# Attention with packed tokens: scores, packed values and projection in eight array tiles of 64 rows by 32 columns

## The chip, the cores and the metric

The program runs on one core of a Trainium2 chip. The metric is device time in microseconds of one execution; less is better. TensorE (PE) does matmuls from a stationary operand (loaded by LDWEIGHTS, shown as PEld) and a moving one; VectorE (DVE), ScalarE (ACT) and GpSimd (POOL) do the rest; SyncE (SP) issues the DMAs.

## The reference

Three layers follow one another, all in f32. B = 8 batches, 8 heads, S = 576 tokens, head size d = 64, 32 packed queries per head.

```
# 1 attention through 32 packed tokens per head
pp  = softmax(p k^T / 8) v            # 32 x 64 per head
x   = softmax(q pp^T / 8) pp          # 576 x 64 per head; heads side by side: 576 x 512
# 2 mixture of 4 causal attention experts (size 64), the best 2 of 4 by x w_gate
out = sum_e gate_e * (causal_softmax((x wq_e)(x wk_e)^T / 8) (x wv_e)) wo_e
# 3 token-shifted feed-forward, y = out, y' = out one token earlier
xk  = mu_k y + (1 - mu_k) y';  xr = mu_r y + (1 - mu_r) y'
res = sigmoid(xr w_r) * (relu(xk w_k)^2 w_v)
```

The kernel never forms x. As x = a2 pp with a2 = softmax(q pp^T / 8), it multiplies the packed values by the weights of layer 2 first (pp w_in, with w_in = all wq, wk, wv and w_gate side by side, 772 columns) and applies a2 to that.

## The kernel before

Heads are worked on in two groups of four (g = 0, 1) per batch; four heads times 32 packed tokens fill 128 partitions. `front(b, g)` is one such group, 16 in all, as a generator of nine steps:

- loads of p, k, v, q on the SP queue (`load`, L231-248);
- scores s1 of the packed queries with the keys (`scores_pair`, the matmul of L224), their maximum (L265) and exp (L270);
- five PE transposes of the result (L277);
- packed values: for each of 5 chunks of 128 keys, 2 matmuls (L286), each for a pair of heads (64 stationary columns, 128 moving ones);
- multiplication by 1/sum and by `bmask` (L293), which zeroes what belongs to the other head of the pair; a PE transpose (L299) gives ppT;
- scores s2 of q with the packed values (`scores_pair` again), a DVE transpose (L306), maximum, subtraction, exp;
- projection: ppT times the weights `wa`, in two column ranges of 512 and 260, 2 matmuls each (L319); ACT writes the rounded result PWh (L325), DVE the rest PWl (L326);
- sums, division and a transpose of a2.

A matmul of the pair form has 128 contracted rows and 64 stationary columns: two heads' 64 features stand on the two halves of the partitions. For s1, p is stored apart, with zeros where the other head's features are; for the packed values the cross products are computed and `bmask` drops them. The two pairs (jj = 0, 1) write PSUM partitions 0-63 and 64-127, so they are two column tiles of the array. `big()` gives a PSUM tile of 2 banks (2 of these), `one()` one of 1 bank (4 of these).

Behind `front` come `values` (L363) and `project` (L418), which apply a2, and per expert `soft` (L477: causal scores, DVE L489, ACT L493), `turn` (PE transposes L516, L523, copied by L211/L213), `pair_out` (L559, L569). `fold` (L706) prepares products of wo with w_k and w_r meanwhile: the weights come in 64-bit form and DVE, ACT and POOL decode them (L622 to L657). Layer 3 follows: `rstage` (L865), `kstage` (L885), `vunit` (L926).

Order: every step of every generator has a due time (constants such as FRONT_T, G1_T, SOFT_T; a batch is 20 units). The steps are called in the order of their due times; some have a priority; then a planner with a model of the instructions' lengths fixes the order on each engine. Each engine runs its list in order.

Of the kernel before, what the change touches and what calls it, by code (L numbers as in the profile page):

```python
# [9 lines left out]
F32 = mybir.dt.float32  # L10
# [4 lines left out]
ALU = mybir.AluOpType  # L15
# [36 lines left out]
def f32(ap):  # L52
    return ap.bitcast(F32)
# [3 lines left out]
def kernel(  # L57
# [3 lines left out]
):  # L61
    nc = tc.nc
    P = 128
    B, NG, _, _, S = q.shape
    D, NPK = p.shape[3], p.shape[6]
    DM, DFF = w_k.shape
    NE, HD = 4, wo.shape[1] // 4
    SH = S // 2
    NT = (S + P - 1) // P
    TAIL = S - (NT - 1) * P  # L70
    QB = 256
# [1 line left out]
    NDT = DM // P  # L73
    QK = 2 * HD * NE
    NCB = S // NPK
    VG = HD * NE + NE
    NQK = QK + VG
    assert w_in.shape == (DM, NQK) and out.shape[2] == DM == NG * 4 * D
    assert (P, S, D, NPK, HD, NE, NT, TAIL) == (128, 576, 64, 32, 64, 4, 5, 64)
    SC = 1.0 / math.sqrt(D)  # L80

# [4 lines left out]
    const = ctx.enter_context(tc.tile_pool(name="const", bufs=1))  # L86
# [7 lines left out]
    def nm(s):  # L94
        uid[0] += 1
        return f"{s}_{uid[0]}"

    def big():
        return psb.tile([P, 1024], F32, tag="big", name=nm("big"))

    def one():
        return pso.tile([P, 512], F32, tag="one", name=nm("one"))

    ident = const.tile([P, P], F32, name="ident")
# [7 lines left out]
    bmask = const.tile([P, 2, D], F32, name="bmask")  # L112
    nc.vector.memset(bmask, 0.0)
    for h in range(4):
        nc.vector.memset(bmask[32 * h : 32 * h + 32, h % 2, :], 1.0)
    lower = const.tile([P, NE, NE], F32, name="lower")
    nc.vector.memset(lower, 0.0)
    for e in range(1, NE):
# [25 lines left out]
    if True:  # L144
# [6 lines left out]
        ex_cm, ex = pool("ex", 2, "left")  # L151
        bt_cm, bt = pool("bt", 1, "left")

        wa = wa_pool.tile([P, NDT, NQK], F32, name="wa")

# [39 lines left out]
                yield  # L195

        def load_wa():
            for c in range(0, NDT, 2):
                nc.sync.dma_start(
                    wa[:, c : c + 2, :], w_in[P * c : P * c + 2 * P].rearrange("(c p) n -> p c n", p=P)  # L200
                )

        def halves(ap):
            return ap.rearrange("p (h n) -> p h n", h=2)
# [12 lines left out]
        def pool_tt(o, x, y, op):  # L217
            nc.gpsimd.tensor_tensor(o, x, y, op=op)  # L218

        def scores_pair(lhs, rhs):  # L220
            ps = big()
            for hf in range(2):
                for jj in range(2):
                    nc.tensor.matmul(  # L224
                        ps[64 * jj : 64 * jj + 64, 512 * hf : 512 * hf + SH],
                        lhs[:, 64 * jj : 64 * jj + 64],
                        rhs[:, jj, SH * hf : SH * hf + SH],
                        start=True, stop=True,
                    )
            return halves(ps)[:, :, :SH]  # L230

        def load(b, gs):

            for g in gs:
                pT = pTs[(b * NG + g) % 2]
                nc.sync.dma_start(pT, p[b, g].rearrange("h d j i n -> (h d) (j i n)"))
                kT = ld.tile([P, 2, S], F32, tag="kT", name=nm("kT"))
                nc.sync.dma_start(kT, k[b, g])
                loaded[b, g] = [pT, kT]
            for g in gs:  # L240
                vn = vns[(b * NG + g) % 2]
                nc.sync.dma_start(
                    vn[:, : NT - 1, :], v[b, g, : (NT - 1) * P].rearrange("(c p) x -> p c x", p=P)
                )
                nc.sync.dma_start(vn[TAIL:, NT - 1, :], v[b, g, (NT - 1) * P :])
                qT = ld.tile([P, 2, S], F32, tag="qT", name=nm("qT"))
                nc.sync.dma_start(qT, q[b, g])
                loaded[b, g] += [vn, qT]

        def front(b, g):  # L250
# [9 lines left out]
                load(b, (g,) if b else range(NG))  # L260
            pT, kT, vn, qT = loaded.pop((b, g))
            yield
            s1 = scores_pair(pT, kT)
            mx = sm.tile([P, 1], F32, tag="mx1", name=nm("mx1"))
            nc.vector.tensor_reduce(mx, s1, op=ALU.max, axis=AX.XY)  # L265
            nb = sm.tile([P, 1], F32, tag="nb1", name=nm("nb1"))
# [30 lines left out]
            yield  # L297
            ps = one()
            nc.tensor.transpose(ps[:, :P], pp, ident)  # L299
# [13 lines left out]
            )  # L313
            nc.scalar.activation(st, st, AF.Exp, scale=SC)
            yield
            ps = big()
            for lo, hi in ((0, QK), (QK, NQK)):
                for jj in range(2):
                    nc.tensor.matmul(  # L319
                        ps[64 * jj : 64 * jj + 64, lo:hi],  # L320
                        ppT[:, 64 * jj : 64 * jj + 64],
                        wa[:, 2 * g + jj, lo:hi],
                        start=True, stop=True,
                    )
# [728 lines left out]
def layout(q, k, v, p, moe_w_gate, moe_wq, moe_wk, moe_wv, moe_wo,  # L1053
           moe2_mu_k, moe2_mu_r, moe2_w_k, moe2_w_v, moe2_w_r):

    import numpy as np

    b, h, _, d = q.shape  # L1060
    ne, dm, hd = moe_wq.shape

    def features(a):
        return a.reshape(b, h // 4, 2, 2, -1, d).transpose(0, 1, 3, 5, 2, 4)

    cols = []
    for e in range(0, ne, 2):
        cols += [moe_wq[e], moe_wq[e + 1], moe_wk[e], moe_wk[e + 1]]
    apart = np.zeros((b, h // 4, 2, d, 2, 2, p.shape[2]), p.dtype)
    for x in range(2):  # L1070
        apart[:, :, x, :, :, x] = features(p)[:, :, x]
    arrays = {
        "q": features(q).reshape(b, h // 4, 2 * d, 2, -1),
        "k": features(k).reshape(b, h // 4, 2 * d, 2, -1),
        "v": v.reshape(b, h // 4, 4, -1, d).transpose(0, 1, 3, 2, 4).reshape(b, h // 4, -1, 4 * d),
        "p": apart,
        "w_in": np.concatenate(cols + list(moe_wv) + [moe_w_gate], axis=1),
        "wo": moe_wo.reshape(ne * hd, dm).T,
        "mu": np.stack([moe2_mu_k, moe2_mu_r]).reshape(2, -1, 128).transpose(2, 0, 1), "w_k": moe2_w_k, "w_v": moe2_w_v, "w_r": moe2_w_r,
    }  # L1080
    arrays = {n: np.ascontiguousarray(a) for n, a in arrays.items()}
    return {n: a.view(np.int64) if a.dtype == np.float64 else a for n, a in arrays.items()}
# [19 lines left out]
```

## Time and profile before

| | |
|---|---|
| median of 3 runs | 822.84 us (822.81 to 822.85) |
| profiled execution | 823.26 us |
| its span | 821.5 us |
| PE busy | 791.0 us, 96% |
| DVE, ACT, POOL busy | 483.9, 480.2, 381.4 us |
| DMA moved | 147.72 MB |

The span goes from the first instruction to the last. Busy time counts an engine's instructions, overlaps once. A chain of waits follows the work that ended last back to its start, at each step to what released it or to the instruction before it on its engine. A matmul's duration runs until its results are written, so matmuls overlap: the pace is read from a run of many. An f32 matmul leaves two records (each LDWEIGHTS and MATMUL), an f32 PE transpose one. `128*64` is rows times columns of the array used. A few matmul records are missing from the trace.

### The profile page before, as it was taken

The numbers are of one execution on the slowest core, as the hardware profiler recorded it, in microseconds if no ns is written. First come the engines' busy times: TensorE is split into PE (matmuls) and PEld (weight loads), VectorE is DVE, ScalarE is ACT, GpSimd is POOL, SyncE is SP. The second block draws the span as 40 slices with busy tenths as digits, with TensorE's granted clock in tenths as the row PEclk, the third lists the DMA queues.
The fourth block names the chain that finished last, engine by engine and source line by source line (L and its number), as shares of the span: only waits on it lengthen the run. The fifth ranks groups of instructions, "written<-read, shape, count | busy, mean of one in ns | idle before, by whom it ended". The sixth has DMA issues, their size and how long they took to land.

```text
span 821.5 us, 13912 instructions
## 1 busy us (share of the span) xinstructions
PE 791.0 (96%) x4800; PEld 639.8 (78%) x4800; DVE 483.9 (59%) x1177; ACT 480.2 (58%) x1093; POOL 381.4 (46%) x490
## 2 busy tenths in 40 slices
PE   7698999999999999999899999999999999999998
PEld 5385968869687796868678888888888888888886
DVE  3989785886868757556856778787584111111111
ACT  2367777687676877778844624232678765556400
POOL 4567666394764735225700407171166443433610
PEclk9899999999999999999999999999999999999999
DMA  9865464634636254112834967785979655555511
GB/s 318 264 158 172 136 199 125 189 125 136 212 106 185 88 138 154 49 50 60 242 106 170 361 243 246 221 264 182 340 260 311 210 198 171 184 162 188 153 66 51
DMA packets 90085, 147.72 MB, mean 180 GB/s; under 512 B 6816, under 2 KB 61600, under 8 KB 87712
## 3 DMA queue, kind: packets, MB, share of 16 engines
q1 hardware_dynamic: 89872, 146.84, 56.2%
q8 instruction: 38, 0.62, 0.3%
q14 instruction: 31, 0.25, 0.1%
q10 hardware_dynamic: 144, 0.00, 0.0%
HBM read 87.04 MB, written 50.33 MB: 167 GB/s over the span
## 4 chain that ended last, share of the span: by engine, by line
PE 76%; DVE 11%; ACT 5%; DMA 4%; issue 2%; POOL 1%; SPq 0%; DVEq 0%; ACTq 0%; POOLq 0%
PE one L926 24%; PE big L885 8%; PE one L885 8%; PE one L559 5%; PE big L418 4%; PE big L865 4%; PE one L865 4%; PE one L706 3%; PE one L363 3%; PE one L477 3%; PE one L516 3%; PE big L224 2%; ACT ms L493 2%; DVE ms L489 2%; DMA raw<-in_w_k_dram 2%
## 5 line engine op out<-in xcount | busy, mean ns | idle before, releaser
L931 DVE TENSOR_TENSOR ring<-one,ring 128x512 f32<-128x512 f32 x36 | 24.9, 691 | 167.1 <-PE one L926 162.4
L926 PE MATMUL one<-wvh,yh 128*128 128x512 f32 x288 | 112.0, 389 | 0.0
L926 PE MATMUL one<-wvl,yh 128*128 128x512 f32 x288 | 112.0, 389 | 0.0
L926 PE MATMUL one<-wvh,yl 128*128 128x512 f32 x288 | 112.0, 389 | 0.0
L493 ACT ACTIVATE ms<-ms,nb 64x64 f32<-64x64 f32 (+4 forms) x160 | 89.5, 560 | 29.2 <-DVE nb L489 26.9
L211 ACT COPY tb<-one 64x128 f32<-64x128 f32 (+5 forms) x208 | 64.6, 356 | 30.3 <-PE one L523 28.0
L218 POOL TENSOR_TENSOR yl<-yvh,yh 128x1024 fp32r<-128x1024 f32 (+1 forms) x24 | 49.4, 2073 | 45.6 <-ACT yh L911 27.7
L637 POOL TENSOR_TENSOR dcx<-dcx,dcu 128x256 f32<-128x256 f32 x40 | 30.6, 764 | 78.2 <-DVE dcu L631 76.8
L559 PE MATMUL one<-tb,vg 128*64 128x320 f32 (+4 forms) x448 | 62.6, 367 | 4.3 <-ACT tb L211 3.4
L926 PEld LDWEIGHTS one<-wvh,yh 128*128 128x128 f32 x288 | 54.1, 188 | 11.3
L926 PEld LDWEIGHTS one<-wvh,yl 128*128 128x128 f32 x288 | 54.1, 188 | 11.3
L926 PEld LDWEIGHTS one<-wvl,yh 128*128 128x128 f32 x288 | 54.1, 188 | 11.0
L489 DVE CUSTOM_DVE_ANT_0 ms<-one,mstrip 64x64 f32<-64x64 f32 (+3 forms) x128 | 51.6, 421 | 15.8 <-PE one L477 13.5
L516 PE MATMUL one<-ident,ms 128*128 128x128 f32 x320 | 55.0, 280 | 2.7 <-ACT ms L493 1.1
L559 PEld LDWEIGHTS one<-tb,vg 128*64 128x64 f32 x448 | 36.9, 138 | 26.5 <-ACT tb L211 6.0
L218 POOL TENSOR_TENSOR yl<-yvl,yh 128x1024 fp32r<-128x1024 f32 x16 | 38.3, 2402 | 37.1 <-issue 19.3
L516 PEld LDWEIGHTS one<-ident,ms 128*128 128x128 f32 x320 | 37.8, 141 | 17.0 <-issue 6.8
L218 POOL TENSOR_TENSOR dt<-cb 128x192 f32<-128x192 f32 (+1 forms) x48 | 29.4, 640 | 35.3 <-ACT p L871 15.5
L477 PE MATMUL one<-ks,qs 128*128 128x64 f32 (+3 forms) x128 | 40.9, 346 | 1.5 <-DMA ks<-ks 1.3
L477 PE MATMUL one<-kl,qs 128*128 128x64 f32 (+3 forms) x128 | 39.2, 306 | 0.0
L1048 ACT ACTIVATE ring<-ring 128x1024 f32<-128x1024 f32 x18 | 19.1, 1060 | 33.7 <-DMA ring<-rscr 33.7
L657 POOL TENSOR_TENSOR wl<-wc,wh 128x256 fp32r<-128x256 f32 x48 | 35.4, 753 | 0.5
(208 smaller groups left out, 2106.4 us busy)
## 6 DMA issues: line engine op xcount, KB each, us to landing
yscr<-y SPq DMA_DIRECT2D x48, 384.0 KB, 3.6
dl<-dscr SPq DMA_DIRECT2D x40, 256.0 KB, 6.1
yvh<-yscr SPq DMA_DIRECT2D x10, 1024.0 KB, 5.5
kT<-in_k_dram SPq DMA_DIRECT2D x16, 576.0 KB, 4.2
qT<-in_q_dram SPq DMA_DIRECT2D x16, 576.0 KB, 5.4
rscr<-rr SPq DMA_DIRECT2D x12, 768.0 KB, 4.8
ring<-rscr SPq DMA_DIRECT2D x36, 256.0 KB, 2.9
out_dram<-ring SPq DMA_DIRECT2D x36, 256.0 KB, 3.2
```

Source lines behind the costliest of these rows:

```text
L211: nc.scalar.copy(o, x)
L218: nc.gpsimd.tensor_tensor(o, x, y, op=op)
L418: nc.tensor.matmul(ps[:, 512 * hf : 512 * hf + SH], ww[:, g, :], xx[:, g, :], start=i == 0, stop=i == 3 * NG - 1,)
L477: nc.tensor.matmul(ps[:, po : po + kn], qs[:, i * P : i * P + P], keys[:, ko : ko + kn], start=x == 0, stop=x == 1,)
L489: nc.vector.tensor_tensor_reduce(halves(mv) if last else mv, sv, halves(mk) if last else mk, op0=ALU.add, op1=ALU.min, scale=-SC, scalar=3 ...
L493: nc.scalar.activation(mv, mv, AF.Exp, bias=nb[p0:], scale=-1.0, accum_out=bat["sums"][p0:, i, e : e + 1],)
L516: nc.tensor.transpose(ps[:, at + j * P : at + (j + 1) * P], ms[:, j * P : (j + 1) * P], ident)
L559: nc.tensor.matmul(av[64 * ee : 64 * ee + 64, qo - lo : hi - lo], vg[:, j, HD * (2 * ep + ee) : HD * (2 * ep + ee + 1)], tslice(tabs[ee], ...
L657: nc.gpsimd.tensor_sub(l, x, f32(h))
L865: nc.tensor.matmul(po, dx[:, NS * t + s, t0 : t0 + P], wpart("r", s, wx, t), start=n == 0, stop=n == 3 * KT - 1,)
L885: nc.tensor.matmul(po.rearrange("p (b n) -> p b n", b=2), wpart("k0" if f < 4 else "k1", s, wx, t)[:, f % 4 * P : f % 4 * P + P], dx[:, :, ...
L926: nc.tensor.matmul(ps, a[:, f, P * t : P * t + P], wres["v"][b][:, f, :], start=n == 0, stop=n == 3 * NFT - 1,)
```

## The change

A helper `eight(lhs, rhs, n)` takes the place of `scores_pair` and of the projection's loop. It issues eight matmuls with 64 contracted rows and 32 stationary columns: for each of the 4 heads j and each half hf of the partitions, one that writes PSUM partitions 32j to 32j + 31, in the bank of that half. The two halves of the partitions hold the two halves of the moving columns (tokens, or columns of the weights: 772 = 2 x 386), and the same 64 features of the head. So p is laid out twice, one copy per half, without zeros; q and k are laid out with tokens 0-287 on the lower and 288-575 on the upper partitions; `w_in` likewise. The packed values are computed per head in four column tiles (128 rows x 32 columns, 64 moving columns), 20 matmuls instead of 10, and nothing has to be masked: `bmask` goes, and the multiplication by 1/sum writes the 64 values twice, so that the transpose gives ppT with both copies. Due times and priorities are as before.

```diff
+        def eight(lhs, rhs, n):
             ps = big()
-            for hf in range(2):
-                for jj in range(2):
+            for j in range(NH):
+                for hf in range(2):
+                    r = slice(64 * hf, 64 * hf + 64)
                     nc.tensor.matmul(
-                        ps[64 * jj : 64 * jj + 64, 512 * hf : 512 * hf + SH],
-                        lhs[:, 64 * jj : 64 * jj + 64],
-                        rhs[:, jj, SH * hf : SH * hf + SH],
+                        ps[NPK * j : NPK * j + NPK, 512 * hf : 512 * hf + n],
+                        lhs[r, NPK * j : NPK * j + NPK],
+                        rhs[r, j, :],
                         start=True, stop=True,
                     )
-            return halves(ps)[:, :, :SH]
+            return halves(ps)[:, :, :n]
...
-            s1 = scores_pair(pT, kT)
+            s1 = eight(pT, kT, SH)
...
             for c in range(NT):
-                for jj in range(2):
+                for j in range(NH):
                     nc.tensor.matmul(
-                        ps[64 * jj : 64 * jj + 64, :P],
-                        aT[:, c, 64 * jj : 64 * jj + 64],
-                        vn[:, c, P * jj : P * jj + P],
+                        ps[NPK * j : NPK * j + NPK, :D],
+                        aT[:, c, NPK * j : NPK * j + NPK],
+                        vn[:, c, D * j : D * j + D],
                         start=c == 0, stop=c == NT - 1,
                     )
-            pp = fr.tile([P, P], F32, tag="pp", name=nm("pp"))
-            nc.vector.scalar_tensor_tensor(
-                pp, ps[:, :P], ri, bmask.rearrange("p a d -> p (a d)"),
-                op0=ALU.mult, op1=ALU.mult,
+            pp = fr.tile([P, 2, D], F32, tag="pp", name=nm("pp"))
+            nc.vector.tensor_scalar(
+                pp, ps[:, :D].unsqueeze(1).to_broadcast([P, 2, D]), ri, None, op0=ALU.mult
             )
...
-            s2 = scores_pair(ppT, qT)
+            s2 = eight(ppT, qT, SH)
...
-            for lo, hi in ((0, QK), (QK, NQK)):
-                for jj in range(2):
-                    nc.tensor.matmul(
-                        ps[64 * jj : 64 * jj + 64, lo:hi],
-                        ppT[:, 64 * jj : 64 * jj + 64],
-                        wa[:, 2 * g + jj, lo:hi],
-                        start=True, stop=True,
-                    )
-            nc.scalar.copy(bat["PWh"][:, g, :], ps[:, :NQK])
-            nc.vector.tensor_sub(bat["PWl"][:, g, :], ps[:, :NQK], f32(bat["PWh"][:, g, :]))
+            ps = eight(ppT, wa[:, NH * g : NH * g + NH, :], NW)
+            nc.scalar.copy(halves(bat["PWh"][:, g, :]), ps)
+            nc.vector.tensor_sub(halves(bat["PWl"][:, g, :]), ps, halves(f32(bat["PWh"][:, g, :])))
```

The tiles that are loaded change shape, not size: pT 128 x 128, kT and qT 128 x 4 x 288 instead of 128 x 2 x 576, wa 128 x 8 x 386 instead of 128 x 4 x 772. `bmask` and its five memsets are removed.

## Rows read from the trace of the kernel before

**Rows 1.** Busy time, share of the span and instructions of each engine (page, part 1).
```profile
PE 791.0 (96%) x4800; PEld 639.8 (78%) x4800; DVE 483.9 (59%) x1177; ACT 480.2 (58%) x1093; POOL 381.4 (46%) x490
```

**Rows 2.** Busy us by stage: length, PE, PEld, DVE, ACT, POOL, clock, DMA share, GB/s.
```profile
20.00:61.00 41.00, 32.62 (x240) 25.50 (x236) 36.83 (x92) 20.65 (x50) 24.96 (x41) 0.92 0.71 213
61.00:103.00 42.00, 39.16 (x303) 31.02 (x302) 34.79 (x105) 30.15 (x88) 28.58 (x43) 1.00 0.51 153
103.00:145.00 42.00, 41.80 (x324) 32.71 (x321) 31.12 (x95) 30.39 (x89) 29.04 (x49) 1.00 0.54 159
145.00:187.00 42.00, 41.52 (x323) 31.34 (x323) 34.22 (x108) 30.53 (x91) 26.67 (x42) 1.00 0.52 155
187.00:229.00 42.00, 41.65 (x336) 33.36 (x335) 33.93 (x108) 31.42 (x91) 25.23 (x45) 1.00 0.60 173
229.00:271.00 42.00, 42.00 (x343) 35.55 (x339) 30.90 (x97) 29.21 (x85) 25.70 (x44) 1.00 0.51 151
271.00:313.00 42.00, 40.68 (x334) 33.81 (x334) 25.16 (x79) 29.68 (x88) 19.95 (x34) 1.00 0.47 134
313.00:355.00 42.00, 40.07 (x313) 31.69 (x313) 28.04 (x90) 33.72 (x99) 15.10 (x25) 1.00 0.26 72
...
430.00:822.00 392.00, 386.95 (x1726) 319.79 (x1726) 171.67 (x248) 187.14 (x253) 146.22 (x96) 1.00 0.63 210
```

**Rows 3.** Chain of waits by line, of 0-21, 103-313, 145-187, 187-229, 313-375 us.
```profile
by line: DMA raw<-in_w_k_dram 51.4%; DMA vn<-in_v_dram 35.5%; SPq L238 4.0%; SPq L236 3.9%; SPq L671 1.8%; issue 1.5%
...
by line: PE one L559 12.5%; PE big L418 10.6%; PE one L706 10.1%; PE one L477 7.6%; PE one L363 7.1%; PE big L224 6.8%; PE one L516 6.7%; PE one L286 4.1%; DVE ms L489 3.4%; ACT ms L493 3.2%; PE big L319 2.8%; DMA raw<-in_w_r_dram 2.7%; PE 
...
by line: DMA raw<-in_w_r_dram 13.3%; PE one L559 9.0%; PE one L477 8.3%; PE big L224 5.3%; PE one L516 4.6%; DVE ms L489 4.0%; issue 3.8%; PE one L363 3.7%; PE big L319 3.4%; DVE kl L437 3.4%; PE one L706 3.4%; PE one L286 3.0%; ACT ms L493
...
by line: PE one L559 15.2%; PE big L418 15.1%; PE one L706 10.6%; PE big L224 8.0%; PE one L477 7.8%; PE one L516 7.7%; PE one L363 7.2%; PE one L286 5.9%; DVE ms L489 5.6%; PE big L477 3.8%; PE big L319 3.4%; PE one L523 2.1%; PE big L569 
...
by line: PE one L559 12.9%; PE big L418 10.3%; PE one L477 7.6%; DVE ms L489 7.2%; ACT ms L493 6.9%; PE one L363 6.1%; PE one L516 6.1%; PE big L224 5.4%; ACT tb L211 5.1%; DMA ks<-ks 3.7%; DVE PWl L326 2.8%; ACT PWh L325 2.4%; PE big L569 
```

**Rows 4.** Pieces of that chain, 187-229 and 313-375 us: start us, us, what.
```profile
194.59 0.55 PE big L277 x5
...
202.79 1.24 PE one L286 x20
...
211.21 1.12 PE big L224 x8
...
216.69 1.45 PE big L319 x8
...
316.56 1.45 PE big L319 x8
...
351.54 1.24 PE one L286 x20
```

**Rows 5.** TensorE in order of time, 75.4-77 us: start us, us, what, count.
```profile
75.22 0.39 PE L559 MATMUL one<-tb,vg 128*64 128x128 f32 x4
75.90 1.19 PE L224 MATMUL big<-kT,pT 128*64 128x288 f32 x8 [0.29 <-DVE nb L489]
```

**Rows 6.** VectorE groups by shape: busy us, mean ns, idle before.
```profile
L326 DVE TENSOR_TENSOR PWl<-big,PWh 128x772 fp32r<-128x772 f32 x16 | 15.2, 949 | 0.1
...
L431 DVE TENSOR_TENSOR l<-big,qs 128x576 fp32r<-128x576 f32 x16 | 12.1, 756 | 9.7 <-ACT qs L430 9.4
...
L293 DVE SCALAR_TENSOR_TENSOR pp<-one,ri,bmask 128x128 f32<-128x128 f32 x16 | 5.5, 344 | 1.2 <-PE one L286 0.9
```

**Rows 7.** DMA issues (page, part 6): count, KB each, us to landing.
```profile
kT<-in_k_dram SPq DMA_DIRECT2D x16, 576.0 KB, 4.2
```

**Rows 8.** 103-430 us, lines L224, L286, L319 alone: us, PE (count), PEld (count).
```profile
103.00:430.00 327.00, 26.48 (x176) 11.68 (x176) 0.99 0.46 135
...
103.00:430.00 327.00, 13.83 (x214) 11.18 (x210) 0.99 0.46 135
...
103.00:430.00 327.00, 18.21 (x96) 5.82 (x96) 0.99 0.46 135
```

More of the change, by code (lines that the diff above doesn't have):

```diff
@@ L63 @@
     P = 128
-    B, NG, _, _, S = q.shape
-    D, NPK = p.shape[3], p.shape[6]
+    B, NG, _, NH, SH = q.shape
+    D, NPK = p.shape[2] // 2, p.shape[4]
+    S = 2 * SH
     DM, DFF = w_k.shape
     NE, HD = 4, wo.shape[1] // 4
-    SH = S // 2
     NT = (S + P - 1) // P
@@ L77 @@
     NQK = QK + VG
-    assert w_in.shape == (DM, NQK) and out.shape[2] == DM == NG * 4 * D
+    NW = NQK // 2
+    assert w_in.shape == (P, NG * NH, NW) and out.shape[2] == DM == NG * NH * D
     assert (P, S, D, NPK, HD, NE, NT, TAIL) == (128, 576, 64, 32, 64, 4, 5, 64)
@@ L111 @@
     )
[L112 to L115, printed above, removed]
     lower = const.tile([P, NE, NE], F32, name="lower")
@@ L152 @@
         bt_cm, bt = pool("bt", 1, "left")
-        wa = wa_pool.tile([P, NDT, NQK], F32, name="wa")
+        wa = wa_pool.tile([P, NG * NH, NW], F32, name="wa")
         qss = [ex.tile([P, TAIL + 2 * S], F32R, name=f"qs{x}", bufs=1) for x in range(2)]
@@ L197, in load_wa @@
         def load_wa():
-            for c in range(0, NDT, 2):
-                nc.sync.dma_start(
-                    wa[:, c : c + 2, :], w_in[P * c : P * c + 2 * P].rearrange("(c p) n -> p c n", p=P)
-                )
+            for c in range(0, NG * NH, NH):
+                nc.sync.dma_start(wa[:, c : c + NH, :], w_in[:, c : c + NH, :])
         def halves(ap):
@@ L235, in load @@
                 pT = pTs[(b * NG + g) % 2]
-                nc.sync.dma_start(pT, p[b, g].rearrange("h d j i n -> (h d) (j i n)"))
-                kT = ld.tile([P, 2, S], F32, tag="kT", name=nm("kT"))
+                nc.sync.dma_start(pT, p[b, g].rearrange("d j n -> d (j n)"))
+                kT = ld.tile([P, NH, SH], F32, tag="kT", name=nm("kT"))
                 nc.sync.dma_start(kT, k[b, g])
@@ L245, in load @@
                 nc.sync.dma_start(vn[TAIL:, NT - 1, :], v[b, g, (NT - 1) * P :])
-                qT = ld.tile([P, 2, S], F32, tag="qT", name=nm("qT"))
+                qT = ld.tile([P, NH, SH], F32, tag="qT", name=nm("qT"))
                 nc.sync.dma_start(qT, q[b, g])
@@ L298, in front @@
             ps = one()
-            nc.tensor.transpose(ps[:, :P], pp, ident)
+            nc.tensor.transpose(ps[:, :P], pp.rearrange("p x d -> p (x d)"), ident)
             ppT = fr.tile([P, P], F32, tag="ppT", name=nm("ppT"))
@@ L315, in front @@
             yield
-            ps = big()
-            for lo, hi in ((0, QK), (QK, NQK)):
-                for jj in range(2):
-                    nc.tensor.matmul(
-                        ps[64 * jj : 64 * jj + 64, lo:hi],
-                        ppT[:, 64 * jj : 64 * jj + 64],
-                        wa[:, 2 * g + jj, lo:hi],
-                        start=True, stop=True,
-                    )
-            nc.scalar.copy(bat["PWh"][:, g, :], ps[:, :NQK])
-            nc.vector.tensor_sub(bat["PWl"][:, g, :], ps[:, :NQK], f32(bat["PWh"][:, g, :]))
+            ps = eight(ppT, wa[:, NH * g : NH * g + NH, :], NW)
+            nc.scalar.copy(halves(bat["PWh"][:, g, :]), ps)
+            nc.vector.tensor_sub(halves(bat["PWl"][:, g, :]), ps, halves(f32(bat["PWh"][:, g, :])))
             yield
@@ L1061, in layout, with features @@
     ne, dm, hd = moe_wq.shape
-    def features(a):
-        return a.reshape(b, h // 4, 2, 2, -1, d).transpose(0, 1, 3, 5, 2, 4)
+    def features(a, n):
+        x = a.reshape(b, h // 4, 4, n, -1, d).transpose(0, 1, 3, 5, 2, 4)
+        return x.reshape(b, h // 4, n * d, 4, -1)
     cols = []
@@ L1068, in layout @@
         cols += [moe_wq[e], moe_wq[e + 1], moe_wk[e], moe_wk[e + 1]]
-    apart = np.zeros((b, h // 4, 2, d, 2, 2, p.shape[2]), p.dtype)
-    for x in range(2):
-        apart[:, :, x, :, :, x] = features(p)[:, :, x]
+    w_in = np.concatenate(cols + list(moe_wv) + [moe_w_gate], axis=1)
     arrays = {
-        "q": features(q).reshape(b, h // 4, 2 * d, 2, -1),
-        "k": features(k).reshape(b, h // 4, 2 * d, 2, -1),
+        "q": features(q, 2),
+        "k": features(k, 2),
         "v": v.reshape(b, h // 4, 4, -1, d).transpose(0, 1, 3, 2, 4).reshape(b, h // 4, -1, 4 * d),
-        "p": apart,
-        "w_in": np.concatenate(cols + list(moe_wv) + [moe_w_gate], axis=1),
+        "p": np.concatenate([features(p, 1)] * 2, axis=2),
+        "w_in": w_in.reshape(h, d, 2, -1).transpose(2, 1, 0, 3).reshape(2 * d, h, -1),
         "wo": moe_wo.reshape(ne * hd, dm).T,
```

1 line of the change is left out of this document (removed).

## The prediction

> **What bounds the kernel now.** I read the page's first part, then busy time by stage, then the chain of waits stage by stage. Over the whole span TensorE is busy 96% [rows 1], but the stages differ, and that decides what faster matmuls are worth [rows 2]. From 430 us on TensorE is busy 386.95 of 392 us on matmuls that the change does not touch: that part can only start earlier. From 103 to 355 us it is busy 40.1 to 42.0 of 42 us, so TensorE time taken away there moves the end. From 20 to 61 us it is busy 32.6 of 41 us, and VectorE 36.8: there VectorE ends the waits. From 61 to 103 us VectorE is still at 34.8 of 42. The chain of waits says the same: until 21 us it is two loads, raw 51.4% and vn 35.5%; from 103 to 313 us it is mostly TensorE, with the scores matmul (L224) at 6.8%, the packed values (L286) at 4.1% and the projection of the packed values (L319) at 2.8% [rows 3]. These three lines are all that the change makes shorter.
>
> **What one column costs.** Five f32 transposes of 128 columns take 0.55 us, 0.11 each, or 0.86 ns per column and record [rows 4]. Each f32 matmul leaves two records. One packed-values step is 20 records of 128 columns; one after the other they would take 2.2 us, and they take 1.24. So the two column tiles of before run at the same time: ten rounds of 0.11 = 1.10 us, and 0.14 over. The same sum gives a scores call (8 records, 288 columns, 4 rounds of 0.247 = 0.99) 0.13 over for its 1.12, and the projection (512 and 260 columns, two rounds each, 1.32) 0.13 over for its 1.45. The rest of 0.13 is what a change of tile shape costs, in and out.
>
> **The change, if all eight tiles run at once.** A scores call becomes 16 records in 2 rounds of 288 columns: 0.49, plus 0.13, plus 0.05 that I allow for eight starts instead of two, 0.67; it saves 0.45 us. The projection becomes 2 rounds of 386 columns, 0.66 + 0.18 = 0.84; it saves 0.61. The packed values become 40 records in ten rounds of 64 columns on four column tiles, 0.55 + 0.19 = 0.74; it saves 0.50.
>
> **How many of them count.** Time off the chain is not counted. From 103 to 313 us the shares are 14.3, 8.6 and 5.9 us of 210; from 313 to 375 us scores are 5.4% of 62 = 3.3, and one packed-values piece (1.24) and one projection piece (1.45) stand on the chain [rows 3, 4]. Together 17.6, 9.8 and 7.3 us, which are 15.7 scores calls, 7.9 packed values and 5.0 projections: 7.1 + 4.0 + 3.1 = 14.2 us. Calls before 103 us are put at nothing: VectorE hides them.
>
> **What takes some of it back.** With VectorE at 83% of a stage (61 to 103 us) the chain there has left TensorE. I take 83% as the point beyond which TensorE time is not worth anything, an estimate. Stage 145 to 187 has 34.22 us of VectorE, so it can't shrink under 41.2; its saving on the chain is 2.0 calls of scores, one projection and one packed value (5.3, 3.4 and 3.0% of 42) = 2.0 us, of which 0.8 is left. Stage 187 to 229 has 33.93, a floor of 40.9; its saving (8.0, 5.9 and 3.4%: 1.35 + 1.0 + 0.6) is 2.95, of which 1.1 is left [rows 2, 3]. That is 3.0 back. The other stages have room (30.9 / 0.83 = 37.2 for 229 to 271).
>
> **Added changes of shape.** Scores share the shape 128*64 with the output matmul L559 now, and 17 times in TensorE's order the two stand beside each other with no change between; the first of them is in the rows [rows 5]. After the change each is a change of shape. At 0.13 us all in, and two thirds on the chain, 1.5 us.
>
> **The rest of the diff.** One DVE multiply of 128x128 with the mask (344 ns, 16 of them) becomes one by a column alone, the input read twice. Nearest is the same row: I take no difference; bounds are 0.15 less each (2.4 us of VectorE in all, of which little is on the chain) and 0.1 more. The two reads of the projection's result now go over two PSUM halves of 386: the DVE row over two halves of 288 takes 756 ns, the one over 772 together 949; the line through them, 0.98 ns per element, leaves nothing for the split. [rows 6] The mask's five memsets go from a start where the chain waits for loads [rows 3]. Loads move the same bytes (k 576 KB) in the same issues on the SP queue, the weights in longer runs [rows 7]: nothing, since the loads before 21 us stay as large and no other queue or order around them changes.
>
> **Sum.** 14.2 - 3.0 - 1.5 = 9.7 us. The profiled execution is 823.26 us (span 821.5 and 1.8 around it), 0.42 over the median of the runs. 823.26 - 9.7 - 0.42 = 813.1: I say 813. Its own range is 807 (nothing given back, no switches, and the pace as above) to 818 (half of the saving).
>
> **What the trace does not show** is whether tiles of 64 rows run at once, whether four column tiles do, and how fast LDWEIGHTS and MATMUL can follow each other. The nearest rows bound it: two column tiles are fully parallel (above), and the densest that the rows have is the packed values, 40 instructions (20 loads, 20 matmuls) in 1.10 us of rounds, 27.5 ns each. I take full parallelism, from the nearest row, and keep the others as rivals.
>
> The Trainium skill (TensorE: Matmul & The Clock Gate, "Measured speedup vs the span model") gives 10.6 times for sixteen tiles at 512 columns, which would carry the sum above; no row here shows row tiles.
>
> **Rivals.**
> *A floor between starts of matmuls.* If matmuls can't start closer than some 25 ns on average, only the packed values notice: 40 starts are 1.0 us against 1.10 now, so 0.1 instead of 0.5 is saved, 0.4 x 7.9 = 3.2 lost: 816. Scores (16 starts, 0.40 of 0.49) and projection stay under it. For it: 64 columns are short. Against: 20 matmuls in 1.10 us start 55 ns apart only because of their columns.
> The Trainium skill (TensorE: Matmul & The Clock Gate) states such a floor under "Wait — 56ns, not 53.3ns?", about 25 ns between starts however few the columns, and under "Measured speedup vs the span model" about 4 ns per tile; by the first the time is 816, by the second 813. It does not say whether the first holds across tiles, and no row here shows it.
>
> *Every instruction has that price: slower.* Loads and matmuls together, two scores calls issue 64 instructions in place of 32, the packed values 80 in place of 40, the projection 32 in place of 16. If loads and matmuls are issued no faster than t, calls on the chain cost 32t, 80t and 32t plus the 0.13: the saving is 15.7(0.99 - 32t) + 7.9(1.10 - 80t) + 5.0(1.32 - 32t) = 30.8 - 1.29t (t in ns). Less 1.5 for the switches it is nothing at 22.7 ns; from there the kernel is slower. At 27.5, the densest of the rows, it costs 6.2: 829. For it: no row is denser. Against: those rows are held back by their columns, not by issue.
>
> *The tiles don't overlap as meant.* If a partition can feed only two streams, the same columns pass per partition as before (1152 in a scores call, both ways): nothing is saved, and the switches cost 1.5: 824. If only the row halves take turns, packed values alone gain: 4.0 - 1.5, 820.
>
> *Nothing is given back, and more.* If the planner pulls TensorE's work ahead, calls off the chain count too: after 103 us 22 scores calls (176 records), 10.7 packed values and 12 projections [rows 8], 9.9 + 5.3 + 7.3 = 22.5, less 1.5: 802.
>
> *The new order puts VectorE in front.* The order is planned anew from other matmul lengths. If the six stages from 103 to 355 us came to leave TensorE idle as the stage from 61 to 103 does (2.84 of 42 us, 17.0 for six, against 4.3 now) 12.7 us would be lost against 9.7 saved: 826. It decides once the six stages' idle time more than triples.
>
> **How the numbers follow.** My forecast 0.50; the floor at 816 0.10; everything gained, 802, 0.12; no overlap 0.12 (824 and 820); price of every instruction 0.06; order 0.10. A measurement of this kernel can't tell under 0.2% (1.6 us, 821.2 to 824.5) from no change. Faster: 0.50 + 0.10 + 0.12 and small parts of the last ones, 0.73; same 0.11, the no-overlap cases mostly; slower 0.16. The range 800 to 825 leaves out 829, half of 826 and what lies under 802.
>
> **What would show it.** Right: L224, L319 and L286 pieces of about 0.67, 0.84 and 0.74 us on the chain, 16, 16 and 40 records each; the stretch behind 430 us as long as now; VectorE's share over 83% in stages around 150 to 230 us. Wrong: a scores call still near 1.1 us (no overlap); packed values at 1.1 (floor) or over 1.24 (price of each instruction); a granted clock under 1.00 behind 103 us, as it is 0.92 from 20 to 61 us where TensorE waits often; or TensorE's idle time from 103 to 355 us over 13 us.

## The result, and the profile after

The changed kernel takes 829.11 us, median of 7 runs (825.41 to 830.50), beside 822.84 of the kernel before (7 runs, 821.78 to 825.42): a ratio of 1.0069, 95% interval 1.0046 to 1.0091. The ratio is that of the means, 5.7 us at 823; the medians differ by 6.3. Forecast were 9.7 us less. The profiled execution is the slowest of its seven: 830.5 us, span 828.7.

The first part of the page of after, busy time by engine, answers to [rows 1].

```profile
PE 774.5 (93%) x5504; PEld 623.5 (75%) x5504; DVE 485.7 (59%) x1172; ACT 479.6 (58%) x1093; POOL 380.8 (46%) x490
```

TensorE is busy 16.5 us less, and yet the span is 7.2 us longer: TensorE is idle for 54.2 us where it was idle for 30.5. So the matmuls did get cheaper, and the question is where 23.7 us of idle time come from. The view of windows of after, with the columns of [rows 2], says in which stages to look.

```profile
20.00:61.00 41.00, 25.15 (x225) 18.17 (x226) 32.30 (x73) 15.15 (x33) 22.27 (x34) 0.64 0.59 180
61.00:103.00 42.00, 38.58 (x425) 31.15 (x423) 35.68 (x107) 33.13 (x98) 30.55 (x47) 1.00 0.51 157
103.00:145.00 42.00, 39.71 (x392) 30.36 (x393) 35.32 (x112) 31.86 (x95) 26.55 (x41) 1.00 0.61 171
145.00:187.00 42.00, 39.38 (x401) 29.73 (x400) 35.07 (x103) 29.31 (x86) 27.18 (x45) 0.96 0.59 169
187.00:229.00 42.00, 41.09 (x429) 33.53 (x427) 33.18 (x106) 29.82 (x87) 24.54 (x43) 1.00 0.55 158
229.00:271.00 42.00, 40.53 (x428) 32.52 (x429) 30.75 (x97) 30.36 (x87) 25.12 (x43) 1.00 0.51 146
271.00:313.00 42.00, 39.70 (x399) 32.12 (x400) 27.30 (x84) 33.31 (x99) 23.40 (x41) 0.96 0.45 129
313.00:355.00 42.00, 39.65 (x427) 31.58 (x428) 29.44 (x94) 32.90 (x100) 16.70 (x27) 1.00 0.34 98
```

From 20 to 61 us TensorE loses 7.5 us of busy time against [rows 2] (25.15 for 32.62), VectorE, ScalarE and GpSimd lose some too, and the granted clock is 0.64 instead of 0.92, so some of the time at the lower of its two levels. That is a start that begins late on every engine. From 103 to 355 us TensorE is idle for 11.9 us in place of 4.3.

**The start.** The timeline of after, 7 to 33 us: start us, us, engine, line, operation, and in brackets the engine's idle time before and what ended it.

```profile
21.96 0.30 DVE L611 TENSOR_SCALAR dce<-raw 128x256 int32<-128x256 int32 x1 [8.07 <-DMA raw<-in_w_k_dram]
...
24.72 0.83 DVE L303 STREAM_TRANSPOSE st<-big 128x288 f32<-128x288 f32 x2
25.48 0.30 DVE L291 TENSOR_SCALAR pp<-one,ri 128x128 f32<-128x128 f32 x1
25.84 0.48 PE L296 MATMUL one<-ident,pp 128*128 128x128 f32 x1 [8.45 <-DVE pp L291]
...
32.39 0.79 ACT L314 CAST PWh<-big 128x772 fp32r<-128x772 f32 x1
```

And the same stretch of the kernel before.

```profile
16.37 0.85 DVE L306 STREAM_TRANSPOSE st<-big 128x288 f32<-128x288 f32 x2 [1.60 <-PE big L224]
17.92 0.34 DVE L293 SCALAR_TENSOR_TENSOR pp<-one,ri,bmask 128x128 f32<-128x128 f32 x1
...
21.29 0.45 DVE L622 TENSOR_SCALAR dce<-raw 128x256 int32<-128x256 int32 x1 [2.36 <-DMA raw<-in_w_k_dram]
21.63 0.79 ACT L325 CAST PWh<-big 128x772 fp32r<-128x772 f32 x1
```

The operations are the same; their order on VectorE is not. Before, the transposes `st` of the first front and the second `pp` came ahead of the first decode of a weight tile (dce), which has to wait for its load. Now the decode stands ahead of both. The load lands at about the same time (21.3 and 22.0 us), so VectorE stands still for 8.07 us with work behind it that needs no load (before, it did that work from 16.4 us on and then waited 2.36 us), TensorE stands still for 8.45 us behind VectorE, and the first projection result (PWh) comes 10.8 us later.

**The middle catches up.** The exp of the first scores (ACT a<-big,nb) starts 11 us late at the third front (43 for 32 us) and 2 us late at the last (338.0 for 335.9). The last PWl starts at 371.7 us in both kernels, so by the end of the fronts nothing is left of the late start. Packing made up for it: with pairs in the same order (below) it starts at 379.1.

**The tail loses again.** SP's queue in after, from the timeline of 445 to 500 us: start us, us, what was issued.

```profile
450.33 0.52 SPq L761 DMA_DIRECT2D dl<-dscr  x1
457.07 0.52 SPq L761 DMA_DIRECT2D dl<-dscr  x1
458.85 3.19 SPq L761 DMA_DIRECT2D wk0l<-wscrk  x4
462.14 2.74 SPq L761 DMA_DIRECT2D wk1l<-wscrk  x4
467.12 3.37 SPq L761 DMA_DIRECT2D dl<-dscr  x3
472.51 3.04 SPq L761 DMA_DIRECT2D dl<-dscr  x3
```

In the kernel before the weights come first, and the last dl load is issued by 470 us.

```profile
451.90 2.14 SPq L772 DMA_DIRECT2D wk0l<-wscrk  x4
454.13 2.62 SPq L772 DMA_DIRECT2D wk1l<-wscrk  x4
458.37 4.37 SPq L772 DMA_DIRECT2D dl<-dscr  x4
465.42 0.52 SPq L772 DMA_DIRECT2D dl<-dscr  x1
467.93 2.06 SPq L772 DMA_DIRECT2D dl<-dscr  x3
```

After, two dl loads stand ahead of the weights, and the other six behind them, issued until 475.55 us. In the chain of waits of after the issue of the weights at 458.85 us follows a store of `rr` (L864) that waits for VectorE; the weights land at 467.1 and the last dl loads on the chain at 477.6 us, and TensorE works on from 478.3. The waits of TensorE in after, 430 to 505 us (engine, tile, line, what it waited for: us in total, times, longest):

```profile
PE big L854 <- DVE rr L839: 2.2, 1, 2.2
PE one L854 <- ACT dh L823: 1.0, 1, 1.0
```

And its window of 470 to 520 us, with the columns of [rows 2]:

```profile
470.00:520.00 50.00, 46.85 (x194) 37.71 (x193) 38.85 (x46) 20.09 (x32) 24.37 (x16) 0.93 0.71 258
```

This window was 50.00 of 50.00 us busy before, at a clock of 1.00. The last cs, the end of layer 2, is 3.1 us late (436.7 for 433.6), the last matmul of `rstage` ends 7.2 us late (498.55 for 491.32), and the span is 7.2 longer.

**The packed calls themselves.** TensorE of after in order of time, about 319 and 353 us.

```profile
318.51 0.72 PE L222 MATMUL big<-qT,ppT 64*32 64x288 f32 x16
319.16 0.55 PE L505 MATMUL one<-ident,ms 128*128 128x128 f32 x3
...
319.75 0.88 PE L222 MATMUL big<-wa,ppT 64*32 64x386 f32 x16
320.56 0.36 PE L466 MATMUL one<-ks,qs 128*128 128x192 f32 x1
...
352.42 0.77 PE L284 MATMUL one<-vn,aT 128*32 128x64 f32 x40
353.11 0.40 PE L466 MATMUL big<-ks,qs 128*128 128x288 f32 x1
```

From the start of a call to the start of what follows it: scores 0.65 us (forecast 0.67, before 1.12), projection 0.81 (0.84, 1.45), packed values 0.69 (0.74, 1.24) [rows 4]. The other calls of after at a clock of 1.00 that nothing holds up take the same within 0.01 us. Each call saves what the forecast says or a little more. This part of it held; what was wrong lies around the calls.

### The profile page after: what moved, and what is told of

It reads as the page before. It is cut to its first block, busy times and chain, and to the rows that moved or that the text cites. A ratio compares the mean times of both kernels' runs of the same rounds, so it can differ in the third digit from the quotient of the medians.

```text
span 828.7 us, 15307 instructions
## 1 busy us (share of the span) xinstructions
PE 774.5 (93%) x5504; PEld 623.5 (75%) x5504; DVE 485.7 (59%) x1172; ACT 479.6 (58%) x1093; POOL 380.8 (46%) x490
## 4 chain that ended last, share of the span: by engine, by line
PE 68%; DVE 13%; DMA 8%; ACT 6%; issue 2%; POOL 2%; SPq 1%; DVEq 0%; POOLq 0%; ACTq 0%
PE one L915 24%; PE big L874 8%; PE one L874 8%; PE one L548 4%; PE big L407 4%; PE one L854 3%; PE one L352 3%; PE one L695 3%; DVE ms L478 3%; DMA dl<-dscr 3%; ACT ms L482 2%; PE one L466 2%; PE big L854 2%; PE one L505 2%; DMA won<-in_wo_dram 1%
## 5 line engine op out<-in xcount | busy, mean ns | idle before, releaser
L548 PE MATMUL one<-tb,vg 128*64 128x320 f32 (+4 forms) x448 | 64.9, 379 | 6.5 <-ACT tb L206 4.3
L478 DVE CUSTOM_DVE_ANT_0 ms<-one,mstrip 64x64 f32<-64x64 f32 (+3 forms) x128 | 51.7, 421 | 18.6 <-PE one L466 16.4
L630 ACT ACTIVATE dcq<-raw 128x256 f32<-128x256 f32 x40 | 17.5, 437 | 42.1 <-DMA raw<-in_w_v_dram 19.2
```

Of the source, the lines that this page charges most:

```text
L478: nc.vector.tensor_tensor_reduce(halves(mv) if last else mv, sv, halves(mk) if last else mk, op0=ALU.add, op1=ALU.min, scale=-SC, scalar=3 ...
L548: nc.tensor.matmul(av[64 * ee : 64 * ee + 64, qo - lo : hi - lo], vg[:, j, HD * (2 * ep + ee) : HD * (2 * ep + ee + 1)], tslice(tabs[ee], ...
```

## The experiments

The theory after the first look: the slowdown is the planner's new order, above all at the start and in the tail; packing alone gains. The rival: packing itself costs it, as sparser matmuls lower the granted clock (mean 0.967 for 0.994).

To separate the two, the order on each engine is taken from a table in place of the planner. The kernels below contain this, and a table of positions per engine:

```diff
         tile_attn_moe_rwkv_kernel(tc, *args)
+        in_order(nc, tc)
...
+    for engine, text in ORDER.items():      # every instruction behind the one listed before it
+            i = on[engine][at]
+            if last is not None:
+                tc.add_manual_dep(i, last.name, why, reason="order")   # order only, no wait
```

Where an order of one matmul form is used for the other, a whole packed group takes the place of the whole group that it replaces.

| kernel | us, median | ratio to before, 95% interval |
|---|---|---|
| pairs, old order (before) | 823.97 / 823.90 / 824.79 | 1 |
| packed, new order (after) | 829.11 | 1.0069, 1.0046 to 1.0091 |
| packed, old order | 819.30 | 0.9942, 0.9921 to 0.9963 |
| pairs, new order | 833.23 | 1.0115, 1.0092 to 1.0138 |
| after, decode moved at the start | 826.14 | 1.0040, 1.0020 to 1.0059 |
| after, old order in the tail | 823.79 | 1.0000, 0.9982 to 1.0017 |
| after, old order at both ends | 820.97 | 0.9962, 0.9945 to 0.9978 |
| packed, old order, early calls twice | 819.18 | 0.9945, 0.9924 to 0.9965 |
| packed, old order, all calls twice | 826.23 | 1.0035, 1.0019 to 1.0051 |
| old order at both ends, early calls twice | 818.20 | 0.9927, 0.9905 to 0.9949 |
| pairs, old order, short maxima | 821.01 | 0.9952, 0.9934 to 0.9971 |
| packed, old order, short maxima | 817.46 | 0.9911, 0.9883 to 0.9939 |
| pairs, old order, half of the exp | 818.83 | 0.9928, 0.9914 to 0.9943 |
| packed, old order, half of the exp | 812.01 | 0.9840, 0.9821 to 0.9859 |

Each ratio is of mean times, to runs of the kernel before on the same chip; after was measured beside 822.84. Compare ratios. In the last four rows a part of the work is left out.

### Form and order apart

Packed matmuls in the old order:

```diff
 # after, with
+ORDER = {...}   # the order of the kernel before, all engines
```

> The changed kernel with every engine's instructions put back into the order that they have in the kernel before (a packed group takes the place of the group that it replaced). Theory ORDER: the packed matmuls save what the prediction summed and the loss comes from the newly planned order alone; then this run is at 809 to 816 us. Rival ARRAY: the packed matmuls themselves cost it (changes of array shape, a lower granted clock because TensorE is less busy); then it is at 823 us or more, with the order of before.

Measured: 819.30, 0.9942. Packing in the order of before saves 0.58%, 4.8 us. That lies between the two ranges: the loss is gone, as the theory of the order asked, but only half of the forecast gain is there.

Pairs in the new order:

```diff
 # before, with
+ORDER = {...}   # the order of after, all engines
```

> The kernel before with every engine's instructions put into the order of the changed kernel. ORDER: the order costs about what separates 813 from 829, and the slower matmuls come on top of 829: 833 to 842 us. ARRAY: the order is harmless and this run stays at 822 to 825 us.

Measured: 833.23, 1.0115, slower, with no packed matmul in it; at the lower end of the range of the order. Its timeline, 7 to 33 us, shows the same start as after:

```profile
20.71 0.29 DVE L622 TENSOR_SCALAR dce<-raw 128x256 int32<-128x256 int32 x1 [5.51 <-DMA raw<-in_w_k_dram]
...
23.46 0.83 DVE L306 STREAM_TRANSPOSE st<-big 128x288 f32<-128x288 f32 x2
24.22 0.30 DVE L293 SCALAR_TENSOR_TENSOR pp<-one,ri,bmask 128x128 f32<-128x128 f32 x1
...
24.58 0.47 PE L299 MATMUL one<-ident,pp 128*128 128x128 f32 x1 [5.95 <-DVE pp L293]
```

So the four corners: the order costs 1.15% with pairs and 1.27% with packed matmuls (1.0069 - 0.9942), 9.5 and 10.5 us; packing saves 0.58% in the old order and 0.46% in the new one. The order is the slowdown, whichever form the matmuls have.

### Where the order costs

The start alone, on VectorE:

```diff
 # the order of after, DVE, about its 18th to 28th instruction
+st L303 (2), m L306, pp L291, st L308
 dce L611, dcx L614, dce L617, dcu L620, dce L611, wc L640   # wc stood ahead of the last st
-st L303 (2), pp L291, m L306, st L308
```

> The changed kernel in its own order but for one move: on VectorE the five instructions that decode the first weight tile stand behind the transposes, the maximum and the subtraction of the first front and the packed values of the second, not ahead of them. START: the 8 us that VectorE waits there for the weights, and the low clock behind it, make the loss: 819 to 823 us. LATE: the fronts had caught up by 340 us in the changed kernel (10 us late at 40 us, 1 us late at 340), so the start is made good anyway and the loss arises near 460 us: 827 to 830 us, with the first 60 us some 8 us shorter all the same.

Measured: 826.14, 1.0040, under after by 0.29%, 2.4 us, which is not clear of the noise (plus or minus 0.30%); it is in neither range. The third exp starts only 1.8 us earlier (41.0 for 42.8). The move mended less than meant: pp comes at 18.76 us again, but the first PWh still at 30.59 (21.63 before), as the transposes of the second front still stand behind decodes (28.93 for 23.29).

The tail alone, and both ends:

```diff
 # after, with
+ORDER = {...}   # tail: after's order up to the last front's packed values, then before's
 # and
+ORDER = {...}   # both ends: before's order to some 69 us, then after's, then before's tail
```

> The changed kernel in its own order up to the packed values of the last front (about 353 us), and from there in the order of the kernel before. LATE: the 4 to 7 us lost between 436 and 498 us, where loads of event blocks wait behind other loads, come back: 821 to 825 us. START: the tail is late because the start is, and 827 to 830 us stays.

> The changed kernel with the order of the kernel before at the start (to about 69 us) and from the packed values of the last front on (about 350 us); between them its own order. Theory ENDS: what the new order costs lies at both ends, and its middle is at least as good as the old one: 814 to 820 us, as with the old order throughout (819) or a little less. Rival EVERYWHERE: the middle of the new order costs as well, which a late start only hides: 821 to 826 us.

Measured: the tail gives back 5.7 us (1.0069 to 1.0000, plus or minus 2.4), as the theory of a late loss asked; both ends 8.8 (0.9962, plus or minus 2.3), on the border of the two ranges, of the 10.5 that the whole old order gives. The start with the tail in order is worth the difference, 3.1 us (plus or minus 2.0). With both ends the window of 470 to 520 us is full again:

```profile
470.00:520.00 50.00, 50.00 (x222) 41.41 (x221) 38.18 (x51) 15.70 (x29) 18.26 (x15) 1.00 0.67 239
```

### The clock

Packed in the old order, the clock is still 0.79 and 0.92 in the first two stages (0.92 and 1.00 before). Does that cost the missing half of the gain? Scores and projection of the first two batches are computed twice, with the same values, and after that those of all batches:

```diff
-        def eight(lhs, rhs, n):
+        def eight(lhs, rhs, n, times=1):
-            for j in range(NH):
+            for j in [j for _ in range(times) for j in range(NH)]:
...
-            s1 = eight(pT, kT, SH)
+            s1 = eight(pT, kT, SH, 2 if b < 2 else 1)     # or 2 always; s2 and the projection alike
```

> The packed kernel in the old order, in which the packed scores and projections of batches 0 and 1 are computed twice (12 groups, the second pass writes the same values over the first), about 8 us more of TensorE work in a stage that VectorE bounds. Theory CLOCK: packing makes TensorE idle so much between 20 and 103 us that it gets a lower clock (0.79 and 0.92 there against 0.92 and 1.00 in the kernel before), and this is where the missing half of the saving went; then the granted clock is back at 0.9 and 1.0 there, and the time is 814 to 818 us, less than 819 with more work. Rival SLACK: the clock in that stage is hidden behind VectorE and changes nothing: 819 to 823 us.

> The packed kernel in the old order with all 48 groups of scores and projection computed twice, so that TensorE's work is about that of the kernel before in an eight-tile form. CLOCK by activity: the mean granted clock returns from 0.98 to 0.99 or more and the time is that of the kernel before, 821 to 825 us. Rival SHAPE: tiles of 64 rows by 32 columns are themselves granted less; the clock stays at 0.985 or under, and the time is 826 us or more.

The windows of packed in the old order, and then of the one with the early calls twice:

```profile
20.00:61.00 41.00, 31.84 (x323) 25.22 (x324) 36.70 (x92) 20.54 (x50) 25.78 (x41) 0.79 0.69 210
61.00:103.00 42.00, 37.50 (x374) 31.13 (x374) 35.03 (x108) 30.80 (x90) 28.33 (x44) 0.92 0.50 153
```

```profile
20.00:61.00 41.00, 33.76 (x456) 26.24 (x446) 36.63 (x92) 21.06 (x51) 25.82 (x41) 0.92 0.69 211
61.00:103.00 42.00, 37.83 (x427) 30.32 (x412) 35.46 (x109) 30.97 (x92) 28.57 (x44) 1.00 0.53 152
```

The clock is back at the level of before, and the time is the same (0.9945 beside 0.9942, each plus or minus 0.21%). VectorE, at 36.7 and 36.6 of 41 us, sets the pace there, so in this pair the lower clock seems paid out of TensorE's spare time, and so the extra work. With all calls twice the mean clock is 0.992, as the theory of activity asked, and the time is 826.23 us, 0.35% above before, as its rival asked: the extra matmuls cost more than the clock returned.

Both ends in the old order together with the early calls twice:

> Old order at the start and at the tail, new order between, and the early groups twice. If ENDS and CLOCK both hold this is the fastest, 811 to 816 us. If CLOCK fails it is where the run with old start and tail is, within 2 us; if ENDS fails it is over 820.

Measured: 818.20, 0.9927, the fastest version that leaves nothing out, and ahead of both kernels; none of the three cases comes true. It can't be told from packed in the old order (0.9942): the intervals overlap. But beside both ends without the extra work (0.9962) it is 0.35% faster, 2.9 us (plus or minus 2.3), with the same order, more work, and a mean clock over its runs of 0.988 for 0.980. So this pair speaks for a price of the clock where the first showed none.

The runs on record speak for it too. Within one kernel the slow executions are those of a low clock (all calls twice: 823.48 us at 0.994, 830.02 at 0.985); over 158 executions, each beside the mean of its kernel, 0.01 less goes with 4.3 us more (plus or minus 0.8). Which of the two brings the other is not shown, as a wait of TensorE can make both.

### Why only half of the gain, in the old order

In the middle of packed in the old order TensorE is idle for longer than before (103 to 355 us, the version with early calls twice):

```profile
103.00:355.00 252.00, 237.04 (x2432) 186.72 (x2431) 184.80 (x569) 184.72 (x540) 140.92 (x235) 0.99 0.48 142
```

That is 15.0 us in place of 4.3 [rows 2]. Its waits of TensorE, 100 to 375 us, are 16.4 us in all: 8.0 for ScalarE's copies and exps, 5.3 for VectorE, 3.1 for a DMA (ks). The longest:

```profile
PE one L548 <- ACT tb L206: 4.0, 3, 2.2
PE one L466 <- DMA ks<-ks: 3.1, 4, 1.9
PE one L505 <- ACT ms L482: 1.5, 3, 0.8
PE one L466 <- ACT tb L206: 1.5, 2, 1.2
```

Two engines are made lighter, each for pairs and for packed matmuls, all in the old order. VectorE, by two maxima over a part of their input:

```diff
-            nc.vector.tensor_reduce(mx, s1, op=ALU.max, axis=AX.XY)
+            nc.vector.tensor_reduce(mx, s1[:, :, :32], op=ALU.max, axis=AX.XY)
...
-            nc.vector.tensor_reduce(m2, st3, op=ALU.max, axis=AX.X)
+            nc.vector.tensor_reduce(m2, st3[:, :, :4], op=ALU.max, axis=AX.X)
```

> Pairs, the old order, and two VectorE maxima of every front over a part of their input: of the first scores over 64 of 576 columns, of the second over 4 of each 32 (any number near the maximum serves a softmax, so only the subtracted number changes). Each takes 0.75 us before; some 1.3 us of VectorE per front go, 21 us in all, some 13 of them between 103 and 355 us. It is the base for the next kernel. Theory (in the old order packing saves half of what it should because TensorE then waits for VectorE): TensorE is idle for only 4 us between 103 and 355 us here, so at most 1.5 us are gained, 822.4 to 824 beside 823.9 of the kernel before. Rival (ScalarE holds it): the same. Rival (neither engine's load, but the places of the instructions in the order): the same.

> Packed, the old order, and the same two maxima over a part. With whole maxima this was 819.3 beside 823.9, 4.6 us saved of the 9.7 forecast, with TensorE idle for some 13 us between 103 and 355 us. Theory (VectorE holds it): at least 3 us more are gained than the pairs gain by the same edit, 814 to 816, and the idle time between 103 and 355 us falls under 9 us. Rival (ScalarE) and rival (places in the order): no more than the pairs gain, 818 to 819.5, idle time 11 to 14.

ScalarE, by the exp of the experts' scores over about half of the columns:

```diff
+                lo = min(kk // 2, max(kk - P, 0))
                 nc.scalar.activation(
-                    mv, mv, AF.Exp, bias=nb[p0:], scale=-1.0,
+                    mv[:, lo:], mv[:, lo:], AF.Exp, bias=nb[p0:], scale=-1.0,
```

> Pairs, the old order, and ScalarE's exp of the experts' scores over about half of the columns (the rest is left as it is, so the output is another): by the slope of its rows, 774 ns at 576 columns and 559 at 320, some 0.6 us less for each of 32 expert and batch pairs, 20 us of ScalarE in all. It is the base for the next kernel. All theories: at most 1.5 us gained, 822.4 to 824; ScalarE's row for L493 falls from some 670 to some 500 ns.

> Packed, the old order, and ScalarE's exp of the experts' scores over about half of the columns (output another). Theory (VectorE holds what packing should have saved): no more than the pairs gain by the same edit, 818 to 819.5. Rival (ScalarE, whose copies and exps end most of TensorE's waits between 100 and 375 us, holds it): at least 3 us more than the pairs gain, 814 to 816, idle time between 103 and 355 us under 9 us. Rival (places in the order): neither this nor the short maxima gain more than 1.5.

Measured, as what packing saves beside pairs with the same edit: 0.58% with whole work (plus or minus 0.21), 0.41% with the short maxima (0.34), 0.88% with half of the exp (0.24). All theories missed one point: the pairs gain by either edit too, 0.48% and 0.72% where at most 1.5 us (0.18%) was expected. With half of the exp they gain it behind the fronts. The last front's PWl and the last cs of the pairs, first before and then with half of the exp:

```profile
371.71 0.96 DVE L326 TENSOR_TENSOR PWl<-big,PWh 128x772 fp32r<-128x772 f32 x1
...
433.62 0.22 DVE L548 RECIPROCAL cs<-cs 128x10 f32<-128x10 f32 x1
```

```profile
371.07 0.96 DVE L326 TENSOR_TENSOR PWl<-big,PWh 128x772 fp32r<-128x772 f32 x1
...
429.36 0.22 DVE L549 RECIPROCAL cs<-cs 128x10 f32<-128x10 f32 x1
```

Up to the last front they are 0.6 us ahead, at the end of layer 2 4.3, the whole difference of the two spans (821.5 and 817.2). So where TensorE is 98% busy a lighter ScalarE gave next to nothing, as expected; the gain is in the stretch behind, where TensorE of before is busy for 70.10 of 75 us (355 to 430).

VectorE's load as the cause falls: taking 1.1 us per front off it (the two maxima fall from 0.75 to 0.22 us each) makes packing worth no more (0.41%, at most 0.75, where that theory asked 0.9). ScalarE's exps are favoured, not shown: packing is worth 7.3 us with half of them, 4.8 with all, but the two intervals overlap; the 2.5 us between them are under the 3 that this theory asked, and the idle time in the middle did not fall to its 9 us. The window of packed with half of the exp:

```profile
103.00:355.00 252.00, 240.22 (x2500) 190.00 (x2506) 190.04 (x583) 176.93 (x554) 145.37 (x241) 0.99 0.49 142
```

It is idle for 11.8 us, within the same stretch of time, but gets more done in it: x2500 matmuls for x2432.

The clock behind 103 us is a rival that no run separates. In the profile of packed in the old order it is 0.96 in three of the six stages from 103 to 355 us and 0.95 from 355 to 430, where before has 1.00 and 0.98. That is some 17 us at the lower of the two levels for 3, and so some 7 us of TensorE's work lost (an estimate: half of the difference, with TensorE busy all through). Three of these falls come right behind a wait of TensorE of 1.85 to 2.25 us (until 273.7, 341.9 and 397.4 us). This profiled execution is the slowest of its six (823.71 us, clock 0.974; the others 0.980 to 0.984), so the usual loss is less. The early calls twice put the clock back at the start only: behind it 0.96 (313 to 355 us) and 0.95 stay.

## Why the prediction was wrong

**The cost of a call** (0.67, 0.84, 0.74) held, at 0.65, 0.81 and 0.69, and with it full parallelism of the eight tiles. The rivals on the array all fall: no overlap (a scores call near 1.1), the price of each instruction (packed values over 1.24), and the floor between starts, as 40 records in 0.69 us start 17 ns apart on average, under the 25 of that rival. The Trainium skill (TensorE: Matmul & The Clock Gate, "Wait — 56ns, not 53.3ns?") says that starts never come closer than about 25 ns; measured over four column tiles together they do.

**The rest of the diff** holds the step that failed: "no other queue or order around them changes". The planner makes the order of the whole program from the lengths of all instructions, so shorter matmuls are also another order, on every engine. That order was priced at nothing in the sum, and costs about 10.5 us of 823 (plus or minus 2.6; 9.5 with pairs). The step before it, "Calls before 103 us are put at nothing: VectorE hides them", was right of the calls (the early calls twice cost no time) and is just why the start is delicate: VectorE is the engine in front there, and the wait that the new order put into its list moved the first projection result by 10.8 us. The same holds for DMA issues on the SP queue in the tail, which the text treated as a stretch that "can only start earlier".

**The rival of the new order** was of the right kind, with 0.10, and had the wrong place. It asked for three times the idle time between 103 and 355 us and got nearly that (11.9 for 4.3); but packed in the old order has as much there (12.8, by 252 less 239.17 us) and is faster than before. Of the 10.5 us, 8.8 came back with the order of the start and the tail.

**The size of the gain** is the second miss. With the order held, packing saves 4.8 us (3.0 to 6.5), not 9.7. Either the term "What takes some of it back", 3.0 us by VectorE's share of 83%, was too small, or the 14.2 us of calls that count too large: the runs show 4.9 us less in all and do not part the two. The signal "TensorE's idle time from 103 to 355 us over 13 us" is there in the version with early calls twice, 15.0. The short maxima speak against the engine that the term named. The other signal, a granted clock under 1.00 behind 103 us, showed too, and the sum has no term for it: the runs of packed in the old order have a mean clock of 0.981, those of before 0.993, and by the 4.3 us per 0.01 above that goes with some 5 us (an estimate), as much as is missing. That the clock is the cause is not shown.

TensorE's busy time is no measure of the saving either: 32 scores calls, 16 projections and 16 packed values save 0.47, 0.64 and 0.55 us each, 34 us in all, and it falls by 16.5. At the lower clock the same call is busy for longer (scores at 26.67 us in after 1.22 us, at 318.51 us 0.72), and from 15.48 to 49.61 us, at 0.50 throughout, after is busy for 16.62 us, of which some 7 would go at the upper level (an estimate by that call). Busy time also counts a matmul until its results are written, 0.22 us for the shortest here, so that short gaps look busy; what that makes was not measured.

34 us less of TensorE's calls are thus 4.8 us less time in the old order, and 5.7 us more with the order that came along.

**Open.** Why the planner put the decode ahead of the first front: its lengths were not taken apart on the chip. What eats the other half of the gain: ScalarE's waits, the DMA of ks and the lower clock behind 103 us are left, and a wait can bring the lower clock with it. Between the start and the tail, some 1.7 us of the order (10.5 less 8.8) was not placed, and is not clear of the noise.

## What to carry to other kernels

Where a planner fixes the order from instruction lengths, a change of one instruction is two changes; run the new instructions in the old order, and the old ones in the new, before either is judged. An instruction that waits for a load belongs behind work that waits for nothing, most of all on the engine that leads a stage: here one decode ahead of two transposes stopped VectorE and TensorE for 8 us, and the new start as a whole cost about 3 us of the time, as the middle caught up. When an edit gains where it should not, look at which landmark the gain first stands in the trace: less exp seemed to help a TensorE 98% busy, and helped behind it.

## What was not expected of the hardware

Eight tiles of 64 rows by 32 columns run fully beside each other: 16 records of 288 columns take 0.65 us with the change of shape, against 1.12 for 8 records in two tiles. The granted clock follows TensorE's work and not the tiles' shape: packed, with the calls once, its mean in the profiled execution is 0.974 (old order; 0.974 to 0.984 over its runs), with the early ones twice 0.990 and with all twice 0.992, beside 0.994 before. The Trainium skill (TensorE: Matmul & The Clock Gate, "Part 1: The HAM clock gate (the "warmup" mystery)") says that activity releases the throttle; the trace agrees. What the clock is worth stays open here: put back from 0.79 to 0.92 in the stage that VectorE leads it returned nothing in the old order (0.9942 and 0.9945), and 2.9 us with both ends in the old order (0.9962 and 0.9927).
